# Linear attention and two expert layers on one core: subtractions on VectorE, masks ahead of a scan, counts with their operands' roles changed

## The chip, the core and the metric

The kernel runs on one NeuronCore of a Trainium2 chip: TensorE for matmuls, VectorE, ScalarE and GpSimd for the rest, SyncE for DMA queues. The metric is the device time of one execution in microseconds. The time before is the median of three runs, 860.9 us (859.4 to 863.0).

## What is computed

The input passes three stages. A linear attention with 32 heads keeps a 48x48 state for each head and decays it by a row of `alpha` at each of 768 steps. Its output, 3072 tokens of 384, is routed to 8 experts: the largest of all token-expert logits are served first, and an expert that has 384 tokens takes no more. A dense layer with squared ReLU follows.

```
for t in range(S):
    state = alpha[:, :, t, :, None] * state + einsum('bhd,bhe->bhde', k[:, :, t], v[:, :, t])
    y[:, :, t] = einsum('bhd,bhde->bhe', q[:, :, t], state)
...
logits = x @ w_gate
for idx in np.argsort(-logits.flatten()):
    tok, e = idx // E, idx % E
    if assigned[tok] >= 0 or counts[e] >= N // E: continue
    assigned[tok] = e; counts[e] += 1
for e in range(E):
    out[assigned == e] = np.maximum(x[assigned == e] @ w1[e], 0.0) @ w2[e]
...
return np.square(np.maximum(x @ w_in, 0.0)) @ w_out
```

## The kernel before

**Attention.** The sequence is cut into chunks of 128 steps, 24 in all (`NS`), two to a unit. For each unit `prep` makes decay factors on VectorE: a forward scan (L143), after which GpSimd multiplies `k` by it (L145), a backward scan (L149), and a product with `q` (L151). For each chunk `scores` multiplies `k` and `q` into one PSUM tile `sc_p`, and VectorE masks it into `am` (L232). `state_mm` makes the state, with an addition on VectorE (L256). `y_mm` adds the part from the state (L274) and the part from the mask (L281) in `y_p`, and ScalarE empties `y_p` (L290). `logits_tok` (L325) and `logits`/`logits_t` make the router's logits; `x_out` transposes `y` (L296) and writes it to DRAM as rows of tokens.

**Order.** Nothing is scheduled automatically: each engine runs its instructions in the order in which the program writes them, and waits by semaphores. Generators (`prep`, `narrow`, `routing`, `w_load`) hand out their work in pieces, one with each `next`. Inside the experts' matmuls `tick` takes one piece of the routing from time to time: one yield asks for the number of ticks until the next piece (`TA`, `TB`), and each tick follows three matmuls.

**Narrowing.** The dense layer's weights come as 64-bit floats. `narrow` turns each of 16 fragments into two 32-bit halves: three bit operations on VectorE (L184, L188, L192), a copy on ScalarE (L196), a subtraction (L200) on the engine in `sub_on`, which is VectorE in the attention and GpSimd from the first expert on. The first expert's weights are split in the same way (L837, L838), with GpSimd for all pieces but three.

**Routing.** One expert is chosen and filled at a time. The keys of all tokens are cut into digits; for each digit a mask `m` says which keys are at least each digit value (`above`, L437), a sum over tokens counts them by expert, and the first digit value at which some expert reaches 384 fixes the next digit's comparison (`x`, `xn`). In routing 0 (`kk == 0`) there are six digits of 6 or 5 bits, and `count` (L443) sums with 24 small matmuls: a mask column block is the standing operand and the one-hot experts `oh` move. In later routings there are eight digits of 4 bits, and `cross` (L457) sums with two wide matmuls and three VectorE steps (L462, L465, L466); routing 1 sums across partitions with a matmul (`total`, L449), the later ones on GpSimd. Routing 0 stands alone between attention and experts, with transposes of the last seven chunks (`x_out`) in its gaps; routing 1 runs inside the first expert's matmuls. `warm(n)` issues matmuls whose result is not used.

**Experts.** For each expert the tokens are gathered, transposed, and multiplied in blocks of nine matmuls of 128x384 (`gemm1` to `gemm4`); each product of two 32-bit operands is three matmuls with high and low halves. `hh`/`hl`, `zh`/`zl` and `gh`/`gl` are the halves of intermediate results, made by ScalarE and VectorE.

Of the kernel before, what the change touches and what calls it, by code (L numbers as in the profile page):

```python
# [25 lines left out]
NS = B * NC  # L26
N = B * S
DM = H * D
E = 8
# [18 lines left out]
WA, WB, W0 = 3, 2, 3  # L48
# [5 lines left out]
def kernel(ctx, tc, q, k, al, v, wg, w1, w2, w_in, w_out, out):  # L54
# [117 lines left out]
    sub_on = [nc.gpsimd]  # L172

    def narrow():

        for f in range(NF2):
# [20 lines left out]
            if sub_on[0] is nc.vector:  # L197
                yield False
            for t, cs in ps:
                sub_on[0].tensor_tensor(w[:, 1, cs], t.bitcast(FT), w[:, 0, cs].bitcast(FT), op=OP.subtract)  # L200
# [66 lines left out]
    def y_mm(s):  # L267
        u, i, c = loc(s)
        f = s % NC == 0
        if not f:  # L270
            for p in range(HP):
                for r in range(2):
                    rr = slice(64 * r, 64 * r + D)
                    nc.tensor.matmul(y_p[side(p, r), r, p // 2, :], st[s - 1][rr, p, :], qs[i][rr, c, p, :],  # L274
                                     start=(p < 2), stop=False, skip_group_check=True)
        if s == NS - 1:
            logits_tok(s - 1, 0)
        for p in range(HP):
            for r in range(2):
                h = 2 * p + r  # L280
                nc.tensor.matmul(y_p[side(p, r), r, p // 2, :], vs[u][:, c, h * D:(h + 1) * D],  # L281
                                 am[s][:, r * HP + p, :], start=(f and p < 2), stop=True, skip_group_check=True)
        if S0 <= s < NS - 2:
# [4 lines left out]
        for g in range(2):  # L288
            rr = slice(64 * g, 64 * g + D)
            nc.scalar.activation(yt[s][rr].rearrange("p (k b) s -> p b k s", b=2),  # L290
                                 y_p[rr, ::(1, -1)[g], :2], AF.Copy)
# [52 lines left out]
    low = mr.tile([128, 32], FH, name="low")  # L344
    spacer = mr.tile([1, 1], FT, name="spacer")

    def route_consts():
# [15 lines left out]
        nc.vector.tensor_copy(left, code)  # L363

# [11 lines left out]
    def warm(n):  # L376

        d = wb[0].rearrange("p a b -> p (a b)")[:, :CAP] if wb[0] is not None else acc[2]
        jf = jc.rearrange("p a b -> p (a b)")
        for _ in range(n):  # L380
            nc.tensor.matmul(d, jf[:, :128], jf[:, 128:128 + CAP], start=True, stop=True)
# [4 lines left out]
    class Keys:  # L386
# [59 lines left out]
        def total(self, i):  # L446
            J = self.J[i]
            tot = rt_p[:, 200:200 + E * J].rearrange("p (e j) -> p e j", e=E)
            nc.tensor.matmul(tot, ones, ex[:, :, :J], start=True, stop=True)  # L449
            return tot  # L450

        def cross(self, i, pe):
# [15 lines left out]
            if pe:  # L468
                return None
# [9 lines left out]
    def routing(kk):  # L479
# [6 lines left out]
        if not last:  # L486
            if kk:
                key = Keys(NARROW)
# [4 lines left out]
                key.digits(0, NS)  # L493
            else:
                key = key0
            x = key.x
            for i, J in enumerate(key.J):
                if kk == 0:
# [631 lines left out]
```

## Time and profile before

| | |
|---|---|
| median of three runs | 860.9 us (859.4 to 863.0) |
| the profiled execution's own time | 862.1 us |
| span of its instructions | 860.3 us |
| TensorE busy | 792.0 us (92%), 5715 matmuls |
| VectorE busy | 542.3 us (63%), 1457 instructions |
| ScalarE busy | 391.4 us (45%) |
| GpSimd busy | 152.3 us (18%) |
| mean granted clock of TensorE | 0.95 |

The span runs from the first instruction to the last. The granted clock is the share of TensorE's full clock that it was given; it has two levels, 1.2 and 2.4 GHz, so 0.5 stands for the lower. A share of busy time over the whole span mixes stages with different limits; the rows below are cut by stage.

### The profile page before, as it was taken

Reading aid. Unit: us, or ns where it says so; the run is one execution under the profiler, and the core shown is the slowest. Engines: PE = TensorE matmul, PEld = TensorE weight load, DVE = VectorE, ACT = ScalarE, POOL = GpSimd, SP = SyncE. Lnnn points to the kernel's source line nnn. Section 1 sums busy time; section 2 is a strip of 40 time slices with the busy share of each in tenths; the row PEclk is TensorE's granted clock in tenths of the full one; section 3 lists DMA queues with packets and bytes.
Section 4 is the critical chain, followed back from the end, with each engine's and each line's share of the span. In section 5 each row is a group of like instructions: output and inputs, shape, how many; then the busy total and the mean of one; then the engine's idle time right before and its main releaser. Section 6 shows DMA issues by size and latency. Waiting matters only on the chain.

```text
span 860.3 us, 15100 instructions
## 1 busy us (share of the span) xinstructions
PE 792.0 (92%) x5715; PEld 744.6 (87%) x5715; DVE 542.3 (63%) x1457; ACT 391.4 (45%) x934; POOL 152.3 (18%) x169
## 2 busy tenths in 40 slices
PE   3778879996787999999999999999999999999996
PEld 2666667765777999999999999999999999999996
DVE  7989988476977676566557656765666553442211
ACT  2456546223243643562455346434624553662443
POOL 3211221014312231012211111220122110101001
PEclk9969979569998999999999999999999999999999
DMA  9868869023000420230032013102300431210000
GB/s 302 217 202 249 255 187 353 35 101 111 1 1 0 124 79 1 74 102 29 1 120 83 1 55 95 54 1 74 102 29 1 124 99 37 83 38 28 1 1 29
DMA packets 32441, 74.78 MB, mean 87 GB/s; under 512 B 4128, under 2 KB 14112, under 8 KB 32368
## 3 DMA queue, kind: packets, MB, share of 16 engines
q1 hardware_dynamic: 25840, 59.65, 22.9%
q0 software_dynamic: 3072, 9.44, 3.2%
q10 hardware_dynamic: 3456, 4.72, 1.6%
q8 instruction: 45, 0.74, 0.4%
q14 instruction: 28, 0.23, 0.1%
HBM read 64.36 MB, written 9.44 MB: 86 GB/s over the span
## 4 chain that ended last, share of the span: by engine, by line
PE 64%; issue 9%; DVE 6%; POOL 1%; ACT 1%; DMA 0%; POOLq 0%; DVEq 0%
PE hu_p L881 10%; PE hu_p L883 10%; PE hu_p L882 10%; PE acc L965 7%; PE acc L966 6%; PE acc L961 6%; PE acc L881 3%; PE acc L883 3%; PE acc L882 3%; PE rt_p L443 1%; DVE nb L192 1%; PE rt_p L457 1%; PE xq_p L874 1%; POOL out_dram L987 1%; DVE nb L184 1%
## 5 line engine op out<-in xcount | busy, mean ns | idle before, releaser
L952 DVE TENSOR_TENSOR gl<-rg,gh 128x384 fp32r<-128x384 f32 x127 | 72.3, 570 | 160.1 <-ACT rg L951 157.6
L949 ACT ACTIVATE rg<-hu_p 128x384 f32<-128x384 f32 x128 | 62.9, 491 | 166.6 <-PE hu_p L883 163.1
L881 PE MATMUL hu_p<-zh,w 128*128 128x384 f32 x384 | 133.3, 347 | 2.2 <-ACT zh L930 2.2
L883 PE MATMUL hu_p<-zl,w 128*128 128x384 f32 x384 | 131.4, 342 | 0.0
L965 PE MATMUL acc<-w,gh 128*128 128x384 f32 x381 | 131.2, 344 | 0.0
L882 PE MATMUL hu_p<-zh,w 128*128 128x384 f32 x384 | 130.3, 339 | 0.0
L966 PE MATMUL acc<-w,gh 128*128 128x384 f32 x381 | 129.2, 339 | 0.0
L961 PE MATMUL acc<-w,gl 128*128 128x384 f32 x381 | 126.2, 338 | 0.0
L916 ACT ACTIVATE hh<-hu_p 128x384 fp32r<-128x384 f32 x64 | 31.4, 491 | 128.1 <-PE hu_p L883 118.1
L471 POOL PARTITION_ALL_REDUCE tot<-ex x40 | 43.0, 1074 | 213.7 <-DVE ex L466 213.7
L881 PEld LDWEIGHTS hu_p<-zh,w 128*128 128x128 f32 x384 | 73.2, 191 | 4.6 <-ACT zh L930 2.5
L917 DVE SCALAR_TENSOR_TENSOR hl<-hu_p,hh 128x384 fp32r<-128x384 f32 x64 | 35.5, 555 | 62.9 <-ACT hh L916 62.8
L883 PEld LDWEIGHTS hu_p<-zl,w 128*128 128x128 f32 x384 | 73.3, 191 | 1.4 <-DVE zl L931 0.3
L882 PEld LDWEIGHTS hu_p<-zh,w 128*128 128x128 f32 x384 | 73.2, 191 | 0.0
L965 PEld LDWEIGHTS acc<-w,gh 128*128 128x128 f32 x381 | 71.8, 189 | 0.1
L966 PEld LDWEIGHTS acc<-w,gh 128*128 128x128 f32 x381 | 71.9, 189 | 0.0
L961 PEld LDWEIGHTS acc<-w,gl 128*128 128x128 f32 x381 | 71.7, 189 | 0.0
L950 ACT ACTIVATE gh<-rg 128x384 fp32r<-128x384 f32 x127 | 66.7, 525 | 4.0
L883 PE MATMUL acc<-hl,w2h 128*128 128x384 f32 x192 | 65.0, 338 | 2.6 <-DVE hl L917 2.6
L881 PE MATMUL hu_p<-xh,w1h 128*128 128x384 f32 x192 | 66.2, 345 | 0.0
L881 PE MATMUL acc<-hh,w2h 128*128 128x384 f32 x192 | 65.9, 343 | 0.0
L883 PE MATMUL hu_p<-xl,w1h 128*128 128x384 f32 x192 | 65.3, 340 | 0.0
(246 smaller groups left out, 1560.1 us busy)
## 6 DMA issues: line engine op xcount, KB each, us to landing
wraw<-in_w_dram SPq DMA_DIRECT2D x62, 384.0 KB, 3.3
raw<-in_w_in_dram SPq DMA_DIRECT2D x16, 384.0 KB, 6.0
raw<-in_w_out_dram SPq DMA_DIRECT2D x16, 384.0 KB, 7.2
vt<-in_v_dram SPq DMA_DIRECT2D x12, 384.0 KB, 5.6
x_d<-xo ACTq DMA_DIRECT2D x24, 192.0 KB, 4.1
a<-in_al_dram SPq DMA_DIRECT2D x9, 451.9 KB, 6.8
k<-in_k_dram SPq DMA_DIRECT2D x9, 448.0 KB, 5.9
q<-in_q_dram SPq DMA_DIRECT2D x9, 448.0 KB, 4.3
```

What stands on the lines that cost most here:

```text
L471: nc.gpsimd.partition_all_reduce(tot[:, :, :J], ex[:, :, :J], 128, bass_isa.ReduceOp.add)
L881: nc.tensor.matmul(dst, wh, xh, start=first, stop=False)
L882: nc.tensor.matmul(dst, wl, xh, start=False, stop=False)
L883: nc.tensor.matmul(dst, wh, xl, start=False, stop=last)
L916: nc.scalar.activation(hh, hp, AF.Relu)
L917: nc.vector.scalar_tensor_tensor(hl, hp, 0.0, hh.bitcast(FT), op0=OP.max, op1=OP.subtract)
L949: nc.scalar.activation(r, up, AF.Relu)
L950: nc.scalar.activation(gh, r, AF.Square)
L952: nc.vector.tensor_tensor(gl, g, gh.bitcast(FT), op=OP.subtract)
L961: nc.tensor.matmul(acc[j], gl[:, j * 128:(j + 1) * 128], wo[f][:, 0, :], start=False, stop=(f == NF2 - 1))
L965: nc.tensor.matmul(acc[j], gh[:, cs], wo[f][:, 0, :], start=(f == 0), stop=False)
L966: nc.tensor.matmul(acc[j], gh[:, cs], wo[f][:, 1, :], start=False, stop=False)
```

## The change

1. All subtractions of `narrow` and all of those of the first expert's weights run on VectorE; `sub_on` goes. `narrow` always has its four pieces, and the pieces are handed out at other places: three at the last chunk of the attention, one for each digit of routing 0, two within the rest of routing 0, one for each block pair of the first expert.
2. In the second chunk of a unit, `scores` (with its mask on VectorE) is written ahead of the backward scan.
3. `y_mm` uses the two halves of its PSUM banks by turns, and the part from the mask comes ahead of the `logits_tok` of the chunk before.
4. `count` has the experts standing and the mask moving, so that counts come out as 8 rows of digit values. A comparison with a sum along each row gives `cm`, and a matmul with the identity `id8` brings the eight sums to all partitions; the largest is `dp`. Routing 1 now counts like this too, with the wide digits; `total` goes.
5. Seven warm-ups ahead of and between the counts go, and four of the twelve at L594.

```diff
-                sub_on[0].tensor_tensor(w[:, 1, cs], t.bitcast(FT), w[:, 0, cs].bitcast(FT), op=OP.subtract)
+                nc.vector.tensor_tensor(w[:, 1, cs], t.bitcast(FT), w[:, 0, cs].bitcast(FT), op=OP.subtract)
...
     def y_mm(s):
         u, i, c = loc(s)
         f = s % NC == 0
+        k0 = s % 2 * 2
...
-                    nc.tensor.matmul(y_p[side(p, r), r, p // 2, :], st[s - 1][rr, p, :], qs[i][rr, c, p, :],
+                    nc.tensor.matmul(y_p[side(p, r), r, k0 + p // 2, :], st[s - 1][rr, p, :], qs[i][rr, c, p, :],
                                      start=(p < 2), stop=False, skip_group_check=True)
-        if s == NS - 1:
-            logits_tok(s - 1, 0)
         for p in range(HP):
...
+        if s == NS - 1:
+            logits_tok(s - 1, 0)
...
         def count(self, i, a, b):
             J = self.J[i]
             for c in range(a, b):
-                nc.tensor.matmul(rt_p[:J, :E], self.m[:, :J, c], self.oh[:, c, :], start=(c == 0),
+                nc.tensor.matmul(rt_p[:E, :J], self.oh[:, c, :], self.m[:, :J, c], start=(c == 0),
                                  stop=(c == NS - 1))
...
-                key = Keys(NARROW)
+                key = Keys(WIDE if kk == 1 else NARROW)
...
+                    cg = mr.tile([128, 64], FH, name="cg")
+                    cm = mr.tile([128, 1], FH, name="cm")
+                    V.tensor_scalar(cg[:E, :J], rt_p[:E, :J], float(CAP), None, op0=OP.is_ge, op1=OP.add,
+                                    accum_out=cm[:E])
+                    yield TA if kk else None
+                    s8 = rt_p[:, 200:200 + E]
+                    nc.tensor.matmul(s8, cm[:E].to_broadcast([E, 128]), id8[:E], start=True, stop=True)
+                    if not kk and i + 1 == key.n:
+                        warm(3)
+                    V.tensor_reduce(dp, s8, axis=AX.X, op=OP.max)
                     if i + 1 < key.n:
-
-                        cm = mr.tile([128, 1], FH, name="cm")
-                        V.tensor_scalar(cg[:J], rt_p[:J, :E], float(CAP), None, op0=OP.is_ge, op1=OP.max,
-                                        accum_out=cm[:J])
-                        yield
-                        nc.tensor.matmul(rt_p[:, 200:201], ones[:J], cm[:J], start=True, stop=True)
...
+                        x = mr.tile([128, NS], FH, name="xn", bufs=2)
+                        V.tensor_scalar(x, key.y, dp, 64.0, op0=OP.subtract, op1=OP.mult)
...
         if kk == 0:
-            warm(12)
+            warm(8)
...
         if c == 0:
             next(pr, None)
             pr = prep(u + 2) if u + 2 < NU else iter(())
-        next(pr, None)
+            next(pr, None)
         if 0 < s < NS - 1:
             scores(s + 1)
+        if c == 1:
+            next(pr, None)
...
         if s == NS - 1:
             key0.above(0, key0.x, 0, NE)
+            for _ in range(3):
+                next(nw)
...
-    warm(2)
     logits_tok(NS - 1, 1)
...
-    warm(WA)
     x_out(next(late))
-    warm(WB)
...
-            (nc.vector if n < 3 else nc.gpsimd).tensor_tensor(fl, got[n], fh.bitcast(FT), op=OP.subtract)
+            nc.vector.tensor_tensor(fl, got[n], fh.bitcast(FT), op=OP.subtract)
```

Line numbers in the rows of the changed kernel are its own: L230 there is L232 before, L254 is L256, L198 is L200, L821 is L838, L900 is L917, L278 is L281, L324 is L325.

VectorE in a unit of the attention, before: `am` is the masked scores, `st` the state, `b_t` the backward scan's result, `nb` and `w` a weight fragment.

```order
L232 TENSOR_TENSOR am<-sc_p,mask 128x1024
L256 TENSOR_TENSOR st_1236<-st_p,st 112x192
L148 RECIPROCAL d_b<-f_t 128x8
L149 SCALAR_TENSOR_TENSOR b_t<-a_83,d_b 128x1032
L232 TENSOR_TENSOR am<-sc_p,mask 128x1024
L192 SCALAR_TENSOR_TENSOR nb<-raw_675,nb 128x768
L200 TENSOR_TENSOR w_1270<-nb,w_1270 128x768
```

VectorE at the same place of the changed kernel:

```order
L230 TENSOR_TENSOR am<-sc_p,mask 128x1024
L254 TENSOR_TENSOR st_1238<-st_p,st 112x192
L230 TENSOR_TENSOR am<-sc_p,mask 128x1024
L148 RECIPROCAL d_b<-f_t 128x8
L149 SCALAR_TENSOR_TENSOR b_t<-a_83,d_b 128x1032
L191 SCALAR_TENSOR_TENSOR nb<-raw_677,nb 128x768
L198 TENSOR_TENSOR w_1272<-nb,w_1272 128x768
```

The second mask has moved ahead of the reciprocal and the backward scan.

VectorE in the first expert's stage, after the keys of routing 1, before: `m` is the mask, `hl` the low half of a block's result, `dg` the digits, `eq`, `cn`, `ex` the sums of `cross`.

```order
L437 TENSOR_TENSOR m<-x_2303,jc 128x360
L184 TENSOR_SCALAR nb<-raw_1475 128x384 x2
L917 SCALAR_TENSOR_TENSOR hl<-hu_p_2098,hh 128x384
L188 SCALAR_TENSOR_TENSOR nb<-raw_1475,nb 128x384 x2
L192 SCALAR_TENSOR_TENSOR nb<-raw_1475,nb 128x384 x2
L917 SCALAR_TENSOR_TENSOR hl<-hu_p_2096,hh 128x384
L404 TENSOR_SCALAR dg<-kb 128x24 x7
L427 TENSOR_SCALAR dg<-dg 128x24
L462 TENSOR_TENSOR eq<-rt_p,own 96x180
L465 TENSOR_REDUCE cn<-eq 96x15
L466 TENSOR_TENSOR ex<-cn,same 96x8x15
```

VectorE there in the changed kernel, with the subtractions of weights (`w2l`, `w1l`) and of a fragment (`w`):

```order
L437 TENSOR_TENSOR m<-x_2306,jc 128x1512
L821 TENSOR_TENSOR w2l<-rg,w2h 128x768
L191 SCALAR_TENSOR_TENSOR nb<-raw_1477,nb 128x384 x2
L900 SCALAR_TENSOR_TENSOR hl<-hu_p_2100,hh 128x384
L821 TENSOR_TENSOR w1l<-rg,w1h 128x768
L198 TENSOR_TENSOR w_2322<-nb,w_2322 128x384 x2
L900 SCALAR_TENSOR_TENSOR hl<-hu_p_2098,hh 128x384
L404 TENSOR_SCALAR dg<-kb 128x24 x5
L427 TENSOR_SCALAR dg<-dg 128x24
L432 TENSOR_SCALAR xd<-x_2306 128x24
L433 SCALAR_TENSOR_TENSOR xd<-dg,xd 128x24
L512 TENSOR_SCALAR cg,cm<-rt_p 8x63
```

The subtractions stand between the results `hl`, the mask is four times as wide, and the three steps of `cross` have become one.

TensorE at the end of the attention, before: `jc` with `y_p` is a warm-up, `kt_p<-wgs` the logits of one chunk by token, `rt_p<-oh,m` a count.

```order
L274 MATMUL y_p<-q_93,st 48x128 x8
L325 MATMUL kt_p<-wgs,yt_109 128x8 x4
L281 MATMUL y_p<-am,vt 48x128 x8
L318 MATMUL rt_p<-ident,lg 128x104 x2
L381 LDWEIGHTS jc
L381 MATMUL y_p<-jc 128x384
...
L325 MATMUL kt_p<-wgs,yt_110 128x8 x4
L443 LDWEIGHTS m
L443 MATMUL rt_p<-oh,m 63x8
```

TensorE at the same place of the changed kernel:

```order
L273 MATMUL y_p<-q_93,st 48x128 x8
L278 MATMUL y_p<-am,vt 48x128 x8
L324 MATMUL kt_p<-wgs,yt_109 128x8 x4
L317 MATMUL rt_p<-ident,lg 128x104 x2
L324 MATMUL kt_p<-wgs,yt_110 128x8 x4
L443 LDWEIGHTS oh
L443 MATMUL rt_p<-m,oh 8x63
```

The logits of the chunk before have moved behind the last part of `y`, the warm-ups are gone, and the standing operand of a count is `oh`.

## Rows read from the trace of the kernel before

**Rows 1.** Busy us by engine and stretch: span, PE, PEld, DVE, ACT, POOL, granted clock, DMA.

```profile
20.00:139.00 119.00, 97.93 (x1461) 77.79 (x1459) 109.79 (x112) 66.32 (x183) 22.62 (x19) 0.87 0.77 231
158.00:198.00 40.00, 35.15 (x258) 26.50 (x257) 24.68 (x98) 9.19 (x23) 4.37 (x5) 0.63 0.26 83
198.00:290.00 92.00, 72.50 (x377) 67.54 (x375) 71.60 (x188) 33.57 (x73) 27.22 (x23) 0.91 0.10 34
290.00:860.00 570.00, 563.28 (x3313) 554.02 (x3312) 310.94 (x1018) 268.45 (x623) 91.09 (x109) 1.00 0.18 53
...
201.00:290.00 89.00, 69.50 (x367) 64.70 (x366) 70.89 (x185) 33.04 (x70) 27.22 (x23) 0.92 0.06 22
```

**Rows 2.** Waits, 198 to 290 us: who waited for whom, us in total, times, longest.

```profile
PE rt_p L449 <- DVE ex L466: 8.3, 3, 5.2
PE rt_p L457 <- DVE m L437: 5.8, 3, 3.1
...
PE acc L883 <- DVE hl L917: 2.6, 1, 2.6
...
PE hu_p L881 <- ACT zh L930: 2.2, 1, 2.2
```

**Rows 3.** Timeline of VectorE, 200 to 300 us: start, us, instruction.

```profile
202.58 1.81 DVE L414 TENSOR_SCALAR kb<-vm 128x24 int32<-128x24 int32 x1
...
206.58 0.17 DVE L404 TENSOR_SCALAR dg<-kb 128x24 int32<-128x24 int32 x1
...
212.43 4.52 DVE L404 TENSOR_SCALAR dg<-kb 128x24 int32<-128x24 int32 x7
```

**Rows 4.** Timeline of GpSimd.

```profile
202.52 1.84 POOL L838 TENSOR_TENSOR w2l<-rg,w2h 128x768 fp32r<-128x768 f32 x1 [7.10 <-ACT w2h L837]
```

**Rows 5.** Groups by line, 198 to 300 us: count, busy us, mean ns, idle before.

```profile
L952 DVE TENSOR_TENSOR gl<-rg,gh 128x384 fp32r<-128x384 f32 x14 | 7.9, 564 | 7.8 <-ACT rg L951 6.1 <-ACT rg L949 1.5
```

**Rows 6.** Timeline of TensorE, 148 to 200 us.

```profile
151.13 0.66 PE L274 MATMUL y_p<-q,st 48*48 48x128 f32 x16 [0.75 <-ACT yt L290]
151.72 1.06 PE L325 MATMUL kt_p<-wgs,yt 128*128 128x8 f32 x8
...
160.74 1.14 PE L381 MATMUL y_p<-jc 128*128 128x384 f16 x3
...
165.87 3.36 PE L443 MATMUL rt_p<-oh,m 128*63 128x8 f16 x24
...
170.52 1.76 PE L443 MATMUL rt_p<-oh,m 128*31 128x8 f16 x24
...
183.43 3.91 PE L381 MATMUL acc<-jc 128*128 128x384 f16 x12
187.26 1.80 PE L630 MATMUL rt_p<-oa,m 128*32 128x12 f16 x24
```

**Rows 7.** Timeline of TensorE in the attention.

```profile
129.18 0.56 PE L248 MATMUL st_p<-vt,kt 128*48 128x48 f32 x16
```

**Rows 8.** Timeline of VectorE at the end of the first routing.

```profile
185.67 0.35 DVE L624 TENSOR_TENSOR m<-pi,jc 128x384 f16<-128x384 int16 x1
```

**Rows 9.** Timeline of all engines in one unit of the attention.

```profile
108.70 1.20 DVE L232 TENSOR_TENSOR am<-sc_p,mask 128x1024 int32<-128x1024 int32 x1
108.92 2.18 POOL L145 TENSOR_TENSOR k<-k,f_t 128x1024 f32<-128x1024 f32 x1 [8.62 <-PE st_p L248]
...
109.82 0.35 DVE L256 TENSOR_TENSOR st<-st_p,st 112x192 f32<-112x192 f32 x1
...
110.00 1.16 PE L230 MATMUL sc_p<-q,k 48*128 48x128 f32 x16 [1.65 <-issue]
...
110.31 2.95 DVE L149 TENSOR_TENSOR_SCAN b_t<-a,d_b 128x1032 f32<-128x1032 f32 x1
```

**Rows 10.** The backward scan's line: ns least, median, most; first and last start.

```profile
L149 DVE TENSOR_TENSOR_SCAN b_t<-a,d_b x14: 695/2946/4028, 4.0 to 134.5; 128x1032 f32<-128x1032 f32 x11, 128x258 f32<-128x258 f32 x2, 128x516 f32<-128x516 f32 x1
```

More of the change, by code (lines that the diff above doesn't have):

```diff
@@ L47 @@
 S0 = NS - 7
-WA, WB, W0 = 3, 2, 3
+W0 = 3
 T0, T1, T2, T3, XF = 5, 4, 5, 5, 11
@@ L376, in warm @@
     def warm(n):
-        d = wb[0].rearrange("p a b -> p (a b)")[:, :CAP] if wb[0] is not None else acc[2]
         jf = jc.rearrange("p a b -> p (a b)")
         for _ in range(n):
-            nc.tensor.matmul(d, jf[:, :128], jf[:, 128:128 + CAP], start=True, stop=True)
+            nc.tensor.matmul(acc[2], jf[:, :128], jf[:, 128:128 + CAP], start=True, stop=True)
     WIDE = (6, 6, 5, 5, 5, 5)
@@ L442, in count, with cross @@
             for c in range(a, b):
-                nc.tensor.matmul(rt_p[:J, :E], self.m[:, :J, c], self.oh[:, c, :], start=(c == 0),
+                nc.tensor.matmul(rt_p[:E, :J], self.oh[:, c, :], self.m[:, :J, c], start=(c == 0),
                                  stop=(c == NS - 1))
[L446 to L452, printed above, removed]
+        def cross(self, i):
             J = self.J[i]
@@ L493, in routing @@
                 key.digits(0, NS)
+                if kk == 1:
+                    key.ahead(1, key.x)
             else:
@@ L532, in routing @@
-                dp = mr.tile([128, 1], FT, name="dp", bufs=2)
-                if kk == 0 and i + 1 < key.n:
-                    x = mr.tile([128, NS], FH, name="xn", bufs=2)
-                    V.tensor_scalar(x, key.y, rt_p[:, 200:201], 64.0, op0=OP.subtract, op1=OP.mult)
+                        yield TB if kk else None
+                    elif not kk:
+                        parts = [(NE, NS)]
+                    for a, b in parts:
+                        key.count(i, a, b)
+                    if not i and not kk:
+                        x_out(next(late))
@@ L541, in routing @@
+                yield TA
+                if i + 1 < key.n:
                     mj = mw.tile([128, 16], FT, name="mj", bufs=1)
@@ L751 @@
     next(r0)
-    for n in (2, 1, 2, 2, 1):
+    for _ in range(len(WIDE) - 1):
         next(r0)
         x_out(next(late))
-        for _ in range(n):
-            next(nw)
+        next(nw)
         next(r0)
-    sub_on[0] = nc.gpsimd
     att.close()
@@ L998, in wstep @@
             w_upto(wdone[0] + 1)
-    wb[0] = None
-    for _ in r0:
-        pass
+    for n, _ in enumerate(r0):
+        if n == 2:
+            for _ in range(2):
+                next(nw)
     for _ in range(W0):
@@ L1020 @@
                 next(wl[0], None)
-                for _ in range(1 + f % 2):
-                    next(nw, None)
+                next(nw, None)
             hn = gemm1(kk, f + 1) if f + 1 < NF1 else None
```

45 lines of the change are left out of this document (11 added, 34 removed).

## The prediction

> **What bounds the kernel now.** I read the busy table by stage first [rows 1]. From 290 us to the end TensorE is busy for 563 of 570 us at the full clock: nothing in this change touches that part, so a microsecond won before it is won at the end, and a microsecond lost there is lost. Three stages come before it. In the attention (20 to 139 us) VectorE is busy for 110 of 119 us and TensorE for 98: VectorE sets the pace. From 158 to 198 us the first routing runs as a chain of small steps, one digit after another, and TensorE's granted clock is 0.63 on average. From 198 to 290 us the first expert's matmuls run, and TensorE is idle for 19.5 of 92 us.
>
> The second view was who TensorE waits for in that last stage [rows 2]: 8.3 us for the `ex` of L466, 5.8 us for the masks `m` of L437, 2.6 for `hl`, 2.2 for `zh`. Sum 18.9 us. The first three are VectorE's. The third view says why VectorE is late [rows 3]: a 24-element `dg` takes 0.17 us at 206.58, but seven of them take 4.52 us from 212.43, and a `kb` of the same size takes 1.81 us at 202.58. Beside that `kb` stands a subtraction on GpSimd that starts at 202.52 and lasts 1.84 us [rows 4]; the two end within 0.05 us of each other. So VectorE stood still until GpSimd was done. These two entries alone hold 1.6 + 3.3 = 4.9 us over the free price. And TensorE pays twice: the granted clock of 201 to 290 us is 0.92 [rows 1], which at two levels of 1.2 and 2.4 GHz means 0.08 x 89 = 7.1 us of work lost; I take it for a consequence of the waits.
>
> **The first expert's stage: subtractions to VectorE.** The change takes five `w1l`/`w2l` subtractions and those of nine weight fragments from GpSimd. GpSimd then has nothing to do in this stage but gathers, and the reason for the long VectorE entries is gone. The price on VectorE is at most 5 x 2 x 0.56 + 9 x 2 x 0.56 = 15.8 us, by the like subtraction of 128x384 at L952 [rows 5]. Against it stand the standstills (4.9 us in two entries alone) and a lighter digit step in routing 1: eight digits with `eq`, `cn`, `ex`, `mj`, `gs`, `xd`, `xn` become six with `cg`, `dp`, `xn` and two steps off the chain. `zh` is freed too: ScalarE's copy of a weight fragment, which waited for VectorE just ahead of `zh`, moves to a later place. What stays: the order on ScalarE now has that copy ahead of the second `hh`, and VectorE emits the keys and the wider masks ahead of the second `hl`, so I leave the 2.6 us of `hl` standing. For places where VectorE, now nearly full, is late again I charge 2.5 us, half way between 0 and 5. So 18.9 + 7.1 - 2.6 - 2.5 = 20.9 us come back before the counts.
>
> **The counts.** Per digit 24 matmuls add up the mask of 128x24 tokens. Before, the mask stands (63 or 31 columns, every 24th element of `m`) and 8 expert columns move: 24 take 3.36 us at 63 columns and 1.76 us at 31 [rows 6], 140 and 73 ns each. After, the experts stand (8 columns, side by side) and 63 or 31 mask columns move. No row shows a moving operand read with such a step, so I bound it. Lower end: at the lower clock twelve warm-up matmuls of 384 columns take 3.91 us [rows 6], 0.85 ns a column, so 63 columns take 53 ns; and no small matmul here is under 35 ns (sixteen of 48 columns in 0.56 us [rows 7]), which holds for 31 columns and for all at the full clock. Upper end: the step costs the moving side what it costs the standing side, 140 and 73 ns. I see no row nearer to one end, and take the middle: 97 and 54 ns at the lower clock, 88 and 54 ns at the full one.
>
> In routing 0 (two digits of 63, four of 31 or 32) this gives 48 x 43 + 96 x 19 ns = 3.9 us less (0 to 7.8). In routing 1 the same 144 matmuls are new work inside a stage where TensorE is to be full: 48 x 88 + 96 x 54 ns = 9.4 us (4.6 to 13.7), less the 16 matmuls of 180 and 8 of 120 columns that go, 3840 columns at half of 0.85 ns, 1.6 us. The first expert's stage is then 20.9 - 9.4 + 1.6 = 13.1 us shorter (8.8 to 17.9).
>
> The Trainium skill (Advanced Engine Details and Errata, Memory Cachelines) says that SBUF has lines of 16 bytes, and that an access to another line each time pays a penalty because it can't hide the memory's latency; it doesn't limit this to the standing operand. The mask's step is 48 bytes, so by that rule flipping the roles saves nothing per matmul and the upper end holds; that is rival 1 below.
>
> **The end of the attention and the first routing.** The chain of TensorE [rows 6]: at 151.13 the last `y` waited 0.75 us for ScalarE to empty the same bank half; with alternating halves that wait has no cause. `logits_tok` of chunk 22 (151.72, 1.06 us) stood ahead of the last L281 and now stands behind it, where it fills the time in which ScalarE empties `y`. Two warm-ups that waited for that emptying go (2 x 0.33 us). Together 2.4 us. The three narrow steps that are put on VectorE here fit ahead of the late logits. Five more warm-ups (the three at 160.74 and two later) stood between the counts of digit 0: 1.6 us. Of the twelve at 183.43 four go; they held L630 (187.26) back, although VectorE's last input for it was ready at 186.02 [rows 8], so 1.2 us. The new step `dp` (a reduce over eight counts, ahead of `xn`) lengthens each of five digits, but a transpose of a late chunk runs on TensorE meanwhile; I charge 1.0 us in all (0 to 1.8). Sum: 2.4 + 1.6 + 1.2 - 1.0 + 3.9 = 8.1 us (4.2 to 12.0).
>
> **Masks ahead of the backward scan.** In a two-chunk unit [rows 9] the forward scan ends, GpSimd multiplies `k` (108.92, 2.18 us), VectorE does the mask of one chunk (108.70), `st` (0.35 us), the backward scan (110.31, 2.95 us), and then the second mask. The scan takes 2.3 us where GpSimd is idle and up to 4.03 us otherwise, median 2.95 [rows 10]; put behind the second mask it comes after GpSimd and saves some 0.65 us. But the second mask needs the scores of 110.00 (1.16 us), and these start only when the first mask has released their bank, at 109.90. The mask can't start before 111.2, and VectorE, the pace-setter, has only `st` to fill 1.3 us with. Net about +0.35 us a unit; in units where VectorE waited for the logits anyhow, nothing. Ten units: +2 us, between 0 (all waits absorbed) and +5 (the scores at the lower clock take twice as long). The early mask lets TensorE run ahead, but TensorE isn't what this stage waits for.
>
> **Sum.** +2.0 - 8.1 - 13.1 = -19.2 us against the profiled execution's own 862.1 us: 842.9. The median of the runs is 1.2 us lower, so 841.7 us.
>
> **Rivals.** 1: the moving mask pays the whole price of its step (140 and 73 ns). For it: the standing mask pays 2.1 ns a column at either clock (the 32-column L630 takes 1.80 us for 24 at the full clock [rows 6], as much as 31 columns at the lower). Against: nothing. Then the sum is +2.0 - 4.2 - 8.8 = -11.0: 850 us. 2: VectorE becomes the bound of the first expert's stage. It is busy for 71.6 of 92 us [rows 1]; take off the standstills, add 15.8 us and take off some 5 us of digit work, and it is left with over 70 us in a stage of 79. If TensorE keeps 13 us of its 26 us of waits and slow clock instead of 5, the time is 850 us. Against: `gl` and `hl` are needed a whole block of nine matmuls after they could be made. 3, slower than before: the step costs the moving side far more than the standing one. With counts at no cost the sum would be -38.4 us; there are 288 of them, so it decides at an average of 133 ns, against 95 ns if both sides pay alike. At double the standing price (190 ns) it is +16 us: 877. Nothing but the missing row speaks for it. 4, the masks do the opposite of what they could: every unit loses 1 us and more, VectorE waiting for scores at a low clock; +8 instead of +2, 848 us.
>
> **How the numbers follow.** My forecast with its own spread (828 to 848) has 0.54, rival 1 0.20, rival 2 0.15, rival 4 0.06, rival 3 0.05. The range from 828 (all lower bounds, no new waits) to 854 (rivals 1 and 2, and +5 in the attention) leaves out rival 3 and mixtures. A measurement of this kernel tells about 0.5% from no change, 4.3 us. Faster by more holds in all but rival 3 and a mixture of 1, 2 and 4: 0.90, within 0.05, slower 0.05.
>
> **What would show it.** Right: no VectorE entry of 24 elements over 0.3 us between 198 and 290; no wait of TensorE for L437 or a count over 1 us there; L443 at 55 to 130 ns a matmul; the backward scan at 2.3 us in each unit with an idle VectorE ahead of the second mask; L630 some 8 us earlier, less the attention's 2. Wrong: L443 as long as before (rival 1), long waits for `hl`, `m` or `gl` with VectorE over 95% busy (rival 2), or an attention that ends more than 5 us later. The forecast falls if the matmuls from the second expert on don't follow at the same distance as before, as all terms rest on that.

## The result, and the profile after

The changed kernel takes 852.8 us (median of four runs, 850.5 to 854.2) against 861.95 of the kernel before, run beside it: a ratio of 0.989, with a 95% interval of 0.985 to 0.993. It is faster, by 9.2 us (1.1%) where 19.2 were forecast. The profiled executions took 862.1 and 852.7 us, their spans are 860.3 and 850.8.

Busy time by stretch, changed kernel, with the columns of [rows 1]. The second stretch runs from the first expert's first matmul to its 487th of 128x384 (counting on into the dense layer and the second expert), from which point on both kernels run evenly to the end.

```profile
20.00:139.00 119.00, 99.67 (x1470) 79.44 (x1468) 103.19 (x112) 66.44 (x183) 22.63 (x19) 0.90 0.77 232
190.44:307.56 117.12, 108.23 (x658) 100.32 (x659) 82.61 (x250) 49.87 (x115) 8.27 (x11) 0.94 0.17 53
```

The same stretch of the kernel before, from matmul to matmul:

```profile
198.16:316.99 118.83, 99.33 (x534) 93.96 (x533) 91.81 (x259) 48.57 (x110) 35.17 (x34) 0.93 0.16 53
```

The first expert starts 7.7 us earlier (190.44 against 198.16), but its stretch is only 1.7 us shorter (117.12 against 118.83), where 13.1 were forecast. TensorE waits 10.6 us less in it (span less busy time: 8.9 against 19.5), and is busy 8.9 us longer. The attention ends where it ended: VectorE's last mask starts at 147.98, before at 148.10.

Whom TensorE waits for in that stretch, changed kernel (columns as in [rows 2]):

```profile
PE acc L944 <- DVE gl L935: 3.2, 4, 1.3
PE acc L864 <- ACT hh L899: 2.4, 1, 2.4
PE xq_p L857 <- DVE xl L839: 2.2, 1, 2.2
PE rt_p L619 <- DVE oa L608: 1.1, 1, 1.1
```

The waits for `ex` and the masks are gone, 14.1 us in [rows 2], and so are those for `hl` and `zh`. Seven others stand in their place, 8.9 us together; of these four lines only that of `oa` made TensorE wait before (0.6 us).

TensorE's timeline, changed kernel (start, us, instruction): the last `y`, counts of 63 and 31 columns in routing 0, the step after the wait for `hh`, and a count of routing 1 at the full clock.

```profile
150.99 0.66 PE L273 MATMUL y_p<-q,st 48*48 48x128 f32 x16 [0.75 <-ACT yt L289]
160.82 2.85 PE L443 MATMUL rt_p<-m,oh 128*8 128x63 f16 x24 [0.18 <-DVE m L437]
165.09 1.52 PE L443 MATMUL rt_p<-m,oh 128*8 128x31 f16 x24
...
199.39 0.69 PE L864 MATMUL acc<-hh,w2h 128*128 128x384 f32 x1 [2.40 <-ACT hh L899]
199.87 0.53 PE L865 MATMUL acc<-hh,w2l 128*128 128x384 f32 x1
...
212.30 2.85 PE L443 MATMUL rt_p<-m,oh 128*8 128x63 f16 x24
```

A count costs 119 ns with 63 moving columns and 63 ns with 31, where the standing mask cost 140 and 73 [rows 6], and as much at the full clock (212.30, granted clock 1.00) as at the lower one (160.82, granted clock 0.50). The matmul after the wait for `hh` takes 0.53 us where 0.33 is usual: the lower clock, until about 209 us (granted clock 0.52):

```profile
199.40:209.70 10.30, 10.30 (x47) 9.03 (x48) 5.91 (x20) 2.85 (x5) 0.00 (x0) 0.52 0.01 2
```

Why `hh` is late, ScalarE and then VectorE around 197 us:

```profile
198.03 0.94 ACT L195 ACTIVATE w<-nb 128x384 fp32r<-128x384 f32 x2 [4.46 <-DVE nb L191]
198.87 0.47 ACT L899 ACTIVATE hh<-hu_p 128x384 fp32r<-128x384 f32 x1
```
```profile
195.25 0.94 DVE L437 TENSOR_TENSOR m<-x,jc 128x1512 f16<-128x1512 f16 x1
196.10 0.95 DVE L821 TENSOR_TENSOR w2l<-rg,w2h 128x768 fp32r<-128x768 f32 x1
196.97 1.02 DVE L191 SCALAR_TENSOR_TENSOR nb<-raw,nb 128x384 uint32<-128x384 uint32 x2
199.37 0.56 DVE L900 SCALAR_TENSOR_TENSOR hl<-hu_p,hh 128x384 fp32r<-128x384 f32 x1 [1.38 <-ACT hh L899]
```

ScalarE's copy of a fragment stands ahead of `hh` in its queue and waits 4.46 us for VectorE's third bit operation, which stands behind routing 1's keys, the wide mask and a subtraction. The same happens near the stretch's end, where the keys of routing 2 stand ahead (VectorE, then ScalarE):

```profile
284.33 0.35 DVE L413 TENSOR_REDUCE vm<-L 128x24 f32<-128x192 f32 x1
...
286.49 0.55 DVE L935 TENSOR_TENSOR gl<-rg,gh 128x384 fp32r<-128x384 f32 x1
...
287.30 1.02 DVE L191 SCALAR_TENSOR_TENSOR nb<-raw,nb 128x384 uint32<-128x384 uint32 x2
288.91 1.03 DVE L198 TENSOR_TENSOR w<-nb,w 128x384 fp32r<-128x384 f32 x2 [0.59 <-ACT w L195]
...
290.19 0.55 DVE L839 TENSOR_TENSOR xl<-xq_p,xh 128x384 fp32r<-128x384 f32 x1
```
```profile
288.35 0.94 ACT L195 ACTIVATE w<-nb 128x384 fp32r<-128x384 f32 x2 [4.41 <-DVE nb L191]
...
289.50 0.47 ACT L838 ACTIVATE xh<-xq_p 128x384 fp32r<-128x384 f32 x1
```

`gl` (286.49) stands behind the keys; `xh` (289.50) stands behind the copy (288.35), `xl` (290.19) behind `xh`, and TensorE waits for both.

### The profile page after: what moved, and what is told of

Its sections match the earlier page's. It is cut to its first block, busy times and chain, and to the rows that moved or that the text cites. A ratio compares the mean times of both kernels' runs of the same rounds, so it can differ in the third digit from the quotient of the medians.

```text
span 850.8 us, 15297 instructions
## 1 busy us (share of the span) xinstructions
PE 796.6 (94%) x5830; PEld 746.2 (88%) x5830; DVE 527.8 (62%) x1454; ACT 391.1 (46%) x934; POOL 124.9 (15%) x146
## 4 chain that ended last, share of the span: by engine, by line
PE 76%; issue 11%; DVE 7%; ACT 2%; POOL 1%; DMA 1%; SPq 0%; POOLq 0%; DVEq 0%
PE hu_p L864 10%; PE hu_p L866 10%; PE hu_p L865 10%; PE acc L948 6%; PE acc L944 6%; PE acc L949 6%; PE acc L864 4%; PE acc L866 3%; PE acc L865 3%; PE sc_p L228 3%; PE rt_p L443 3%; PE y_p L278 3%; PE xt_p L295 1%; PE y_p L273 1%; PE kt_p L237 1%
## 5 line engine op out<-in xcount | busy, mean ns | idle before, releaser
L899 ACT ACTIVATE hh<-hu_p 128x384 fp32r<-128x384 f32 x64 | 31.4, 491 | 142.2 <-PE hu_p L866 142.2
L900 DVE SCALAR_TENSOR_TENSOR hl<-hu_p,hh 128x384 fp32r<-128x384 f32 x64 | 35.6, 556 | 67.5 <-ACT hh L899 67.4
L934 ACT ACTIVATE rg<-rg 128x384 f32<-128x384 f32 x128 | 65.1, 509 | 0.0
```

Of the source, the lines that this page charges most:

```text
L900: nc.vector.scalar_tensor_tensor(hl, hp, 0.0, hh.bitcast(FT), op0=OP.max, op1=OP.subtract)
L934: nc.scalar.activation(g, r, AF.Square)
```

## The experiments

Each kernel but the sixth starts from the changed one. Times are medians beside the kernel before on the same chip (861.9 to 863.0 us), ratios with their intervals. The attention varies from profile to profile even where the code up to there is the same: VectorE's last mask starts between 146.5 and 150.6 us in the changed kernel and the seven of its variants that differ only later (runs 1, 3, 4, 5, 8, 9, 12). What an edit to the first expert does is therefore read in the stretch. Each kernel has one profile, and the stretch isn't quite fixed either: in run 7, whose code there is the changed kernel's, it takes 118.5 us against 117.1, so a difference of 1.4 us in it tells nothing. The table at the end of this section accounts for the stretch; the expectations call its row of long matmuls the slow clock.

**1. The copy behind `hh`.**

```diff
             if kk == 0:
                 next(wl[0], None)
-                next(nw, None)
             hn = gemm1(kk, f + 1) if f + 1 < NF1 else None
+            if kk == 0:
+                next(nw, None)
```

> The changed kernel, with one edit: in the first expert's first loop the weight fragment's piece is handed out after gemm1 and not ahead of it, so that ScalarE's copy of a fragment (0.94 us) stands behind hh. Theory A: the 2.40 us that TensorE waits for hh at 197, and the stretch at the lower clock that follows it (199.4 to 209.8 us, about 4.7 us lost), both come from that copy, which waits for VectorE's keys of routing 1. Both go: about 7 us less than the changed kernel's 852.8, some 846 us, and TensorE's granted clock is 1.0 from the first block on. Rival B: VectorE is the bound of this stage whatever ScalarE does; the wait moves to hl, to a mask or to a count, and less than 2 us are won (851 to 853 us).

849.75 us, 0.986 (0.983 to 0.988). TensorE's timeline at the place that waited for `hh`:

```profile
198.33 0.33 PE L864 MATMUL acc<-hh,w2h 128*128 128x384 f32 x1
198.51 0.34 PE L865 MATMUL acc<-hh,w2l 128*128 128x384 f32 x1
199.04 0.45 PE L866 MATMUL acc<-hl,w2h 128*128 128x384 f32 x1 [0.20 <-DVE hl L900]
199.33 0.34 PE L864 MATMUL acc<-hh,w2h 128*128 128x384 f32 x1
```

Wait and slow stretch are gone: from the 28th to the 55th matmul this kernel gains 5.0 us on the changed one. It had lost 1.5 us before, the lower clock holding until 193.6 in its first block, where the changed kernel has the full one, and loses 1.1 after 288. Net 2.8 us. A is right on the cause, and less came of it than A said.

**2. The mask in rows.** `jr` holds the digit values once; the mask's index is chunk first, digit value second.

```diff
+            if self.rows:
+                nc.vector.tensor_tensor(self.mc[:, a:b, :J], x[:, a:b, None].to_broadcast([128, b - a, J]),
+                                        jr[:, None, 1:J + 1].to_broadcast([128, b - a, J]), op=OP.is_ge)
+                return
...
-                nc.tensor.matmul(rt_p[:E, :J], self.oh[:, c, :], self.m[:, :J, c], start=(c == 0),
+                nc.tensor.matmul(rt_p[:E, :J], self.oh[:, c, :], self.mc[:, c, :J], start=(c == 0),
```

> The changed kernel, with the mask of routings 0 and 1 written with the digit values of one chunk side by side (128 x chunk x 64 instead of 128 x 64 x chunk), so that the moving operand of a count is read without a step; everything else as it is. Theory A: the step is what a count's column costs (119 ns for 63 columns, 63 ns for 31). Then 63 columns take 30 to 55 ns and 31 columns some 30 to 35 ns, the counts in the first expert's stage fall from 11.4 to 5 or 6 us and those of routing 0 by some 5 us: about 10 us less than 852.8, so 843 us, less what the mask costs more on VectorE. Rival B: a moving column of a count costs about 1.9 ns with or without a step; 119 and 63 ns stay, and the time stays at 852 to 854 us.

845.5 us, 0.980 (0.977 to 0.984). Two counts of routing 0 on TensorE's timeline, and VectorE's groups of masks from 140 to 300 us (count, busy us, mean ns, idle before):

```profile
161.89 1.65 PE L451 MATMUL rt_p<-m,oh 128*8 128x63 f16 x24 [0.58 <-DVE m L442]
...
165.89 0.93 PE L451 MATMUL rt_p<-m,oh 128*8 128x31 f16 x24 [0.18 <-DVE m L442]
```
```profile
L442 DVE TENSOR_TENSOR m<-x,jr 128x1512 f16<-128x1512 f16 x1 | 1.7, 1728 | 0.0
```

A count fell to 69 and 39 ns at the lower clock, and those of routing 1 from 11.4 to 4.6 us in all. So the step of 48 bytes made 50 of the 119 ns at the lower clock, and 83 at the full one, where 63 columns now take 36 ns (last section). VectorE pays: 1.73 us for the mask of 128x1512, against 0.94. That took most of routing 0's gain (41.8 us from the last mask to the first expert, against 42.5) and made the wait for `hh` 3.2 us; the stretch is 7.8 us shorter. A:

```profile
190.76:300.11 109.35, 99.68 (x659) 92.68 (x659) 85.25 (x250) 49.76 (x115) 8.27 (x11) 0.97 0.18 57
```

**3. Narrow digits in routing 1.**

```diff
-                key = Keys(WIDE if kk == 1 else NARROW)
+                key = Keys(NARROW)
```

> The changed kernel with routing 1 on the eight 4-bit digits (15 or 16 columns moving, 192 counts) instead of six digits of 6 and 5 bits (63 and 31 columns, 144 counts). Theory A: a count costs 4 ns and 1.9 ns a column, so 15 columns take 33 to 40 ns and the counts of this routing 6.5 to 7.7 us instead of 11.4, and VectorE writes 2900 instead of 6000 mask elements a partition; two more digits of about 7.2 us each lengthen the routing from about 257 to 271 us, still ahead of the work that needs it: 848 to 850 us. Rival B: a count has a floor of 60 ns and more, or the longer routing makes the gather late: 853 us and more.

850.1 us, 0.987 (0.984 to 0.991). 192 counts of 15 or 16 columns took 5.9 us, 31 ns each: A, and a little under its price. Up to the 217th matmul the kernel is 10.0 us ahead of the changed one; then masks and `oa` come late (2.9 and 2.6 us of waits), and 2.5 us remain. The two more digits met the rest of VectorE's work.

**4. and 8. Pieces in another order.** The fourth run hands out one piece ahead of `gemm3` and one behind it; the eighth one more at the first block pair, so that a subtraction no longer follows its copy directly.

```diff
+            if kk == 0:
+                next(nw, None)
             if f + 1 < NF2:
                 gn = gemm3(z, f + 1)
...
             if kk == 0:
                 next(nw, None)
-                next(nw, None)
```

> The changed kernel, with one edit: in the first expert's second loop the two pieces of a weight fragment that are handed out together are handed out apart, one ahead of gemm3 and one behind it. Theory A: VectorE's wait of 0.59 us for ScalarE's copy (seven times), and ScalarE's copy that waits for VectorE's third bit operation with rg and xh queued behind it, are what makes gl and xl late between 257 and 292 us; TensorE's 6.5 us of waits and 1.5 us of slow clock there shrink by 3 to 6 us: 847 to 850 us. Rival B: VectorE has simply too much work there (23.8 of 30 us busy from 270 to 300): less than 1 us is won, 852 to 854 us.

```diff
                 next(nw, None)
                 next(nw, None)
+                if f == 0:
+                    next(nw, None)
```

> The changed kernel, with one piece of a weight fragment more at the first block pair of the first expert's second loop, so that the pairs of pieces are (2,3) and (4,1) and not (3,4) and (1,2): the subtraction no longer stands right behind ScalarE's copy that it waits for. Theory A: VectorE's seven waits of 0.59 us go, gl and xl come earlier, and TensorE's 6.5 us of waits from 257 to 292 us shrink by 3 us or more: 847 to 850 us. Rival B: what counts is ScalarE's copy, which waits for VectorE's third bit operation with rg, gh and xh queued behind it; two bit operations now stand ahead of it, so as much or more is lost: 853 to 858 us.

858.75 us, 0.996 (0.994 to 0.998), and 858.5, 0.997 (0.994 to 0.9995): both 6 us slower than the changed kernel (4 of them in the stretch), both against A. Waits of TensorE from 257 to 300 us, fourth run, then eighth:

```profile
PE acc L948 <- ACT gh L933: 4.1, 2, 2.7
PE acc L944 <- DVE gl L935: 2.5, 4, 1.3
```
```profile
PE acc L948 <- ACT gh L933: 2.3, 3, 1.0
PE acc L944 <- DVE gl L935: 2.5, 4, 1.5
```

`gh` is new: the copy now stands ahead of ScalarE's three steps of a block. Of VectorE's seven waits of 0.59 us none is left in the fourth run and one in the eighth, so they were not what made TensorE wait. The new waits stand behind the copy.

**5. Fragments' subtractions on GpSimd.**

```diff
-                nc.vector.tensor_tensor(w[:, 1, cs], t.bitcast(FT), w[:, 0, cs].bitcast(FT), op=OP.subtract)
+                (nc.gpsimd if fine[0] else nc.vector).tensor_tensor(w[:, 1, cs], t.bitcast(FT),
+                                                                    w[:, 0, cs].bitcast(FT), op=OP.subtract)
```

> The changed kernel, with the subtractions of the weight fragments (L198) back on GpSimd from the first expert on; those of the first expert's own weights stay on VectorE. Theory A: of VectorE's work it is this (1.03 us and a wait of 0.59 us for ScalarE's copy, each time) that makes gl and xl late between 257 and 292 us; without it TensorE's 6.5 us of waits and some 1.5 us of slow clock there fall to 1 or 2 us, as before, and GpSimd's standstills of VectorE cost little there: 846 to 849 us. Rival B: the standstills come back and cost as much as they did before (long entries of VectorE, TensorE waiting for masks and counts): 853 to 860 us.

856.5 us, 0.994 (0.992 to 0.997). The waits are those of the changed kernel (3.3 us for `gl`, 2.2 for `xl`, 1.9 for `hh`, 0.9 for `oa`), and the stretch is 118.3 us, 1.2 longer, no more than it varies by; another 2 us of the loss lie ahead of the edit. VectorE is busy for 80.4 us of the stretch, 2.2 less than in the changed kernel, though subtractions of 9.2 us left it: the standstills took the room (B), but TensorE waits for no mask and no count, as B had it. So this run does not show what the fragments' subtractions cost; A fell, as nothing was won by moving them.

**6. The subtractions of part 1 alone, on the kernel before.** The pieces are handed out where they were before.

```diff
-    sub_on[0] = nc.gpsimd
...
-            (nc.vector if n < 3 else nc.gpsimd).tensor_tensor(fl, got[n], fh.bitcast(FT), op=OP.subtract)
+            nc.vector.tensor_tensor(fl, got[n], fh.bitcast(FT), op=OP.subtract)
```

> The kernel before, with part 1 alone: the subtractions of narrow and of the first expert's weights all on VectorE, nothing else changed. Theory A (the prediction's): GpSimd's subtractions made VectorE stand still, and the standstills made TensorE wait for ex and m; without them the 19.5 us of waits and 11.9 us of slow clock in the first expert's stage fall by 10 us and more together: 848 to 852 us. Rival B: VectorE, with the subtractions on it, is late in the same places; less than 4 us are won: 857 to 862 us.

852.5 us, 0.989 (0.986 to 0.992): as fast as the whole change. Its stretch, and whom TensorE waits for there:

```profile
198.06:305.12 107.06, 95.63 (x533) 90.11 (x534) 89.96 (x283) 48.37 (x110) 8.20 (x11) 0.97 0.18 59
```
```profile
PE rt_p L449 <- DVE ex L466: 3.7, 4, 1.3
PE rt_p L457 <- DVE m L437: 2.2, 4, 0.6
PE rt_p L633 <- DVE oa L622: 2.0, 1, 2.0
PE hu_p L880 <- ACT zh L929: 1.3, 1, 1.3
```

A: 11.8 us of the stretch come from the subtractions, 8.1 of them waits. This profile is of the fastest of the four executions (850.3 us); by the medians the subtractions are worth 9.4 us of the whole time. `ex` and the masks still make TensorE wait, 5.9 us instead of 14.1.

**7. The scan ahead of the second mask again.**

```diff
-            next(pr, None)
+        next(pr, None)
         if 0 < s < NS - 1:
             scores(s + 1)
-        if c == 1:
-            next(pr, None)
```

> The changed kernel, with part 2 undone: the backward scan ahead of the second mask again. Theory A: the scan that is 0.65 us shorter behind the mask and VectorE's wait for the scores ahead of it cancel; VectorE's busy time from 20 to 139 us goes up from 103 to about 110 us, the attention ends within 1 us of the changed kernel's, and the time stays at 852 to 854 us. Rival B: the order wins or loses 2 us and more by itself: 849 to 851 or 855 to 857 us.

851.4 us, 0.988 (0.985 to 0.991). VectorE's waits for the scores from 20 to 139 us, changed kernel, then this one:

```profile
DVE am L230 <- PE sc_p L228: 13.4, 10, 2.2
```
```profile
DVE am L230 <- PE sc_p L228: 2.2, 1, 2.2
```

VectorE is busy for 113.1 of the 119 us, against 103.2 (it gets through five instructions more here; runs 10 and 11, with the same order, show 109.8 and 110.0): what the shorter scans save, the waits for scores take. This execution's attention ended 2.8 us earlier, but those of runs 10 and 11, with the same order, ended 1 us later than the changed kernel's (last mask at 149.2 and 148.95). The order's own effect is under what these runs resolve. The stretch, whose code is that of the changed kernel:

```profile
187.96:306.50 118.54, 109.98 (x659) 101.81 (x659) 82.64 (x250) 49.86 (x115) 8.27 (x11) 0.93 0.17 53
```

**9. Routing 1 as before** (with `total` and the second argument of `cross` restored).

```diff
-                key = Keys(WIDE if kk == 1 else NARROW)
+                key = Keys(NARROW)
...
-                if kk < 2:
+                if kk == 0:
...
-                cp = key.cross(i)
+                cp = key.cross(i, kk == 1)
                 yield TA
+                if kk == 1:
+                    cp = key.total(i)
```

> The changed kernel, with routing 1 alone as before: eight 4-bit digits, cross with total, no counts. All other parts stay. Theory A: the counts of routing 1 (11.4 us of TensorE, and the wide masks ahead of hh) cost the first expert's stage about 10 us more than cross does once the subtractions are on VectorE; the stage (first matmul of the first expert to the point where both kernels run evenly) shortens from 117.1 to about 107 us: 842 to 845 us. Rival B: cross with its three VectorE steps and two digits more makes TensorE wait for VectorE again, and wins less than 4 us: 849 to 853 us.

845.85 us, 0.981 (0.978 to 0.984). The stretch:

```profile
193.25:303.80 110.55, 96.43 (x534) 91.03 (x533) 88.67 (x278) 48.44 (x110) 8.00 (x11) 0.96 0.18 56
```

A, smaller: 6.6 us shorter, 5.2 us more waits against 10.7 us less of counts.

**10. Runs 1, 2 and 7 together.**

> The changed kernel with three edits tried singly: ScalarE's copy of a fragment behind hh, the masks of routings 0 and 1 in rows, the backward scan ahead of the second mask. Theory A: they act in different places and add up, 3.1 + 7.3 + 1.4 us: 840 to 842 us. Rival B: the waits that one takes away come back in the other (the wider masks in rows, 0.8 us longer on VectorE, ahead of hl or a count): 844 us and more.

844.1 us, 0.980 (0.976 to 0.984), where B begins. The stretch is 10.4 us shorter, as much as the gains of 1 and 2 in it add up to (2.8 and 7.8); part of the waits came back as B says (1.5 us for `cg`, 1.0 for a mask, 1.0 for `hl`).

**11. Two pieces for each block of the first loop,** on top of run 10.

```diff
             if kk == 0:
                 next(nw, None)
+                next(nw, None)
             w_upto(15 + 3 * (f // 2))
```

> The kernel of the three edits, with two pieces of a weight fragment for each block of the first expert's first loop instead of one, so that the fragments are all narrowed some four block pairs earlier in the second loop. Theory A: TensorE's 6.5 us of waits and 1.5 us or more of slow clock between the 266th and the 410th matmul come from the fragments' pieces that meet the second expert's weights and the keys of routing 2 on VectorE and ScalarE; the last four of these six waits shrink by half or more: 2.5 to 5 us less than the three edits alone. Rival B: the first loop is now late instead (VectorE is busy 27.8 of 45.6 us there, and more pieces stand between masks and hl): no gain, or a loss of 1 to 3 us.

842.8 us, 0.978 (0.975 to 0.981), not to be told from run 10. Both theories are right in their halves: the waits at the 344th matmul and ahead of it stay, the last three are gone, and the part from the 262nd matmul on is 4.5 us shorter; the part before it is 4.4 us longer. These two kernels beat both the one before and the changed one.

**12. One bit operation left out.**

```diff
-            for t, cs in ps:
+            for t, cs in ps if fine[0] is None else ():
                 nc.vector.scalar_tensor_tensor(t, raw[:, cs, 1], 0xC0000000, t, op0=OP.bitwise_and,
                                                op1=OP.bitwise_or)
```

> The changed kernel, with the second of the three bit operations of narrow (L187, 1.02 us for a fragment) left out from the first expert on, so that about seven weight fragments lack their sign and top exponent bit; the order of everything else stays. Theory A: VectorE's amount of work is the bound of the first expert's stage; with some 7 us less of it there TensorE's 8.9 us of waits and 9.7 us of slow clock fall by 4 us or more together, above all the waits for gl and xl from the 266th matmul on: 844 to 849 us. Rival B: not the amount but the order is what makes TensorE wait (the copy ahead of hh, the keys of routing 2 ahead of the third bit operation); the six late waits stay within 1 us in sum, and the time is 851 to 853 us.

850.7 us, 0.988 (0.985 to 0.992), between the two theories. With eight operations of 1.02 us left out VectorE is busy for 75.4 us of the stretch, 7.2 less, and TensorE waits 2.4 us less. The stretch itself, 115.9 us, is 1.2 shorter, no more than it varies by. The waits of 0.39 (twice) and 1.04 us for `gl` are gone; those for `xl` (2.2 us), `hh` (2.0) and `oa` (1.1) stand:

```profile
PE xq_p L857 <- DVE xl L839: 2.2, 1, 2.2
PE acc L864 <- ACT hh L899: 2.0, 1, 2.0
PE rt_p L619 <- DVE oa L608: 1.1, 1, 1.1
PE acc L944 <- DVE gl L935: 1.0, 1, 1.0
```

So a quarter of the waiting comes from the amount; the rest stays, as B says of the order.

**The stretch accounted for,** in us, from start to start of TensorE's matmuls: gaps over 0.08 us are waits; what an expert's matmul takes beyond 0.174 us, where that is over 0.08 us, goes into long matmuls; counts take in what follows them (`id8`, or `cross` and `total`). Long matmuls are partly the clock and partly matmuls that stand next to a wait or a count: run 10 has 5.5 us of them at a granted clock of 1.00. What the clock took is estimated in the row below, as (1 - granted clock) x span from the rows above.

| | before | 6: subtractions alone | 9: routing 1 as before | changed | 2: rows | 10 |
|---|---|---|---|---|---|---|
| waits | 19.5 | 11.4 | 14.1 | 8.9 | 9.7 | 10.1 |
| long matmuls | 11.9 | 8.4 | 8.8 | 9.7 | 8.0 | 5.5 |
| (of these, the lower clock) | (8.3) | (3.2) | (4.4) | (7.0) | (3.3) | (0.0) |
| counts | 1.4 | 1.3 | 1.4 | 12.1 | 5.2 | 5.0 |
| the rest | 86.0 | 85.9 | 86.3 | 86.5 | 86.4 | 86.2 |
| sum | 118.8 | 107.1 | 110.6 | 117.1 | 109.4 | 106.7 |

## Why the prediction was right and wrong

The direction was right, and the time lies in the range, 11 us above the forecast. Half of the forecast gain was missing, and all that was missing was in one stretch.

**Attention: in the range, but not resolved.** +2.0 (0 to +5) was said, -0.1 measured; but the attention's end varies by 4.2 us between profiles of the same code, so no run here tells +2.0 from nothing. The steps are the ones described: the scan takes 2.31 us in every two-chunk unit but one (2.91), against a median of 2.95 [rows 10], and VectorE waits for the scores in ten units (13.4 us, run 7).

**End of the attention and first routing: right in sum.** -8.1 was said, -7.6 measured (from the last mask to the first expert). The 2.4 us ahead of the counts came as 2.7, but not by the path described: the wait of 0.75 us on the last `y` [rows 6] is still there, at 150.99, now for the emptying of the other half of the same banks, so "has no cause" was wrong. Why it still waits for that was not tried. The warm-ups came out as said. Counts saved 2.0 us, not 3.9 (2 x 0.51 and 4 x 0.24), and `dp` cost less than 1.0: a 31-column digit takes 2.91 us where it took 3.05, 0.10 less of a gain than its count alone.

**First expert's stage: the failing step.** -13.1 was said, -1.7 measured. By the table, waits and long matmuls fell by 12.8 us (31.4 to 18.6) where 20.9 were to come back: 8.1 of the missing 11.4 us. Of these, 4.9 are the clock's term (7.1 said; long matmuls fell by 2.2, the clock's part of them by 1.3) and 3.2 the waits (13.8 said, 10.6 measured). The counts cost 10.7 us more where 7.8 were said, 2.9 more; the rest is 0.5. So the step that failed first is the sum of 20.9 us: it let all of the clock and all but 5.1 us of the waits come back. By its terms:

- The price of a count. I took the middle between the free and the full step, 9.4 us in routing 1; it was 11.4. (By the floor of 35 ns the lower bound of 4.6 us should have been 5.0; the floor itself was too high, as run 3's counts took 31 ns.) The moving mask pays 85% of what the standing one paid, so rival 1 was nearer, and a row of before spoke for it: the 2.1 ns a column at either clock. Run 2 shows the step to be the cause of most of the price at the full clock. The Trainium skill (Advanced Engine Details and Errata, Memory Cachelines) says so of any access that goes to another line each time, and this case agrees for the moving side: 119 ns with the step, 69 without, for 63 columns at the lower clock.
- "18.9 + 7.1 - 2.6 - 2.5 = 20.9 us come back". The standstill was read rightly, and run 6 shows its worth: 11.8 us of the stretch, waits and long matmuls together, where my sum before the counts had 20.9. What was mis-sized was the 2.5 us for a VectorE that is late again: after the change 8.9 us of waits remain, not 5.1. Of these, 2.4 us stand at the very copy that moved ahead of the second `hh`. I had named its place and left the price of `hl` standing there; the price was right, and the slow clock behind it was not counted (run 1 won 5.0 us there).
- "7.1 us of work lost" to the clock "I take it for a consequence of the waits". It can be one (run 1 takes away a wait and the slow stretch behind it), but it doesn't go as the waits go: run 10 keeps 10.1 us of waits at a granted clock of 1.00. In the changed kernel the waits are 10.6 us less, and the lower clock still took about 7.0 us, 8.3 before.
- "From 290 us to the end [...] nothing in this change touches that part". It does: `narrow` has four pieces where it had three from the first expert on, and fewer are handed out early, so fragments are still being narrowed when the second expert's weights and the keys of routing 2 come. From the 262nd matmul to the 487th the kernel before waits 0.6 us, the changed one 6.5; the changed kernel is 16.3 us ahead of before at 266 us of its own span, and 9.4 at 308. Run 11 puts pieces earlier and takes 3.6 us of these waits away, but loses as much ahead of them; no run here hands them out without a price.

So the balance of the stretch is: subtractions -11.8 (run 6), the first routing's side and the later pieces +3.5 (run 9 against 6), the counts of routing 1 +6.6 (changed against run 9). Each is a difference of two single profiles, good to some 2 us by my estimate (1.4 us in run 7; run 6's profile is 2.2 us under its median). The last two are 10.1 us: the change won 7.6 us in the first routing and 11.8 with the subtractions, and gave back half of that here.

**The rivals.** Rival 1 was the nearer by its price (routing 0 saved 2.0 us, where it had none), rival 2 by its effect: VectorE is not busy all the time (82.6 of 117 us), but what it does stands in an order in which ScalarE's copy, and behind it `hh`, `gh` or `xh`, waits for it. Each forecast 850 us by itself, and that the time is near 850 is in part luck: about half of rival 1 came (2.9 us here and 1.9 in routing 0, of 8.2) together with what rival 2 had charged (8.1 us, of 8), though not by its reason, and in the attention +2.0 did not show. Rivals 3 and 4 did not come. Of what I said the profile would show, no VectorE entry of 24 elements takes over 0.35 us, TensorE waits for no mask or count of routing 1, and a count lies between 55 and 130 ns; the waits for `gl` that were to speak for rival 2 came with VectorE at 71%, not over 95%.

## What to carry to other kernels

When work moves to an engine that has room, look at who stands behind its new neighbours in the queues of the others: a copy on ScalarE that waits for VectorE holds everything behind it, and taking one such place away won 5.0 us there (2.8 us in the whole stretch). Swapping the roles of a matmul's operands left 85% of the price of a strided read here; lay the data out so that the columns lie side by side, and see what that costs the engine that writes them. And test each part of a change alone: the subtractions alone were as fast here as all five parts together, because another part gave its gain back.

## What the runs showed of the hardware

After a wait of TensorE the length of the wait doesn't tell what the granted clock does. The wait of 2.40 us for `hh` was followed by the lower clock until about 209 us. After one of 3.19 us at the same place in run 2 the lower clock came later and for 3.4 us, and after one of 1.81 us in run 3 not at all (run 2, then run 3 from the end of its wait):

```profile
202.40:205.80 3.40, 3.40 (x24) 3.29 (x20) 3.33 (x16) 0.00 (x0) 0.00 (x0) 0.50 0.00 0
```
```profile
199.39:250.00 50.61, 47.67 (x415) 43.14 (x415) 34.97 (x111) 20.71 (x42) 0.00 (x0) 1.00 0.00 1
```

In run 10 waits of 1.0, 1.5 and 1.0 us left the clock of the whole stretch at 1.00, with 10.1 us of waits in it:

```profile
190.64:297.36 106.72, 96.66 (x659) 89.74 (x659) 85.05 (x250) 50.01 (x115) 8.71 (x11) 1.00 0.18 59
```

Moving columns that are 48 bytes apart cost some 1.9 ns each at either clock (2.85 us for 24 x 63 at both), while 63 columns side by side cost 69 ns at the lower clock and 36 ns at the full one (run 2, TensorE's timeline in routing 1):

```profile
210.01 0.86 PE L451 MATMUL rt_p<-m,oh 128*8 128x63 f16 x24
```
